# Linear attention and a token/channel mixer in one kernel: the engines' orders and PSUM banks drawn anew for the end of batch 0, batch 1 and the maps of batch 2

## The chip, the core and the metric

The kernel runs on one core of a Trainium2 chip. A core has a matrix engine (TensorE, PE below; its weight loads are listed as PEld), a vector engine (VectorE, DVE), a scalar engine (ScalarE, ACT), a general engine (GpSimd, POOL) and an engine that here only issues transfers (SyncE, SP). Each takes its instructions strictly in the order in which the program gives them; semaphores order them among one another. SBUF is the on-chip memory, PSUM the eight banks of 2 KB in each partition that PE writes its products to. The metric is the device time of one execution in microseconds (us).

## What is computed

Eight batches of 576 rows; q, k and v have 8 heads of 64 columns. Cut to what matters:

```python
def phi(x): return np.where(x > 0, x, np.exp(x) - 1.0) + 1.0
q_p, k_p = phi(q), phi(k)
kv  = einsum('bhsd,bhse->bhde', k_p, v);  z = k_p.sum(axis=2)
x   = (q_p @ kv) / (q_p @ z + 1e-6)            # heads side by side: 576 x 512 a batch
h   = np.maximum(x.T @ w_tok1, 0) @ w_tok2     # mixes rows: 576 -> 256 -> 576
u   = x + h.T
out = u + np.maximum(u @ w_ch1, 0) @ w_ch2     # mixes columns: 512 -> 1536 -> 512
```

Inputs and output are float32; inside, matmuls work on bfloat16.

## The kernel before

One stage follows another for each batch, and the stages of neighbouring batches are interleaved. Every piece of work is a named step; `ORDER` (L64) is the list of all 1085 names, and the loop at the end (L1165) emits them in that order. So it fixes each engine's order: two steps on different engines may stand in either order in the list without a difference, two on the same engine may not. `BANK` (L40) says in which PSUM bank each product lies; two products with one bank can't be in flight together, the second waits until the first has been read.

A name is the batch, the step, and its part. Those that the text uses, n being the batch:

- nLq0, nLk1, nLv0 ...: loads of half of q, k or v, issued by SP (L226, 576 KB each). `GATE` (L32) holds 2Lq0 back until B0 has landed, and 4Lq0 until 2uT1 has.
- nkx0, nqx1: the exponential of phi on ACT (L250); nka0, nqa1: max(x+1, 1) on DVE (L254); nkb0, nqb1: the smaller of both on DVE (L260). There is one buffer for the second (`ybuf`), so nka1 waits for nkb0. nv0, nv1: cast of v (L273), on ACT or, for those in `ON_DVE`, on DVE.
- nK: kv on PE (L300, 72 small matmuls); nKc0, nKc1: its copies on ACT (L306).
- 1Q00 to 1Q11 with 1Qc..: PE transposes of q in batch 1 and their copies (L318, L324); later batches transpose by DMA, nqT0 and nqT1 (L333, SP).
- 1n00 to 1n21 with 1nc..: batch 1's numerator and denominator on PE and the division on DVE (L350, L359 to L362); nn: the same for a later batch in one step of 40 matmuls (L385), divided by nnd, nne, nn0, nn1, nn2, no0, no1 (L398 to L420).
- nf0, nf1 with nfr0, nfr1: first product of the row mixer and its relu on ACT (L446, L450). 1h.. with 1hu.., 1g2 with 1gu2, ng0, ng1 with ngu0, ngu1: its second product and the sum u (L457, L468). 1t0 to 1t3 with 1tc0 to 1tc3: transposes of u by PE; nuT0, nuT1: by DMA (L487).
- 0ma, 0mb, 1ma, 1mb with a number from 0 to 11: the two halves of a map, the first product of the column mixer (L684, two matmuls of 512 columns each). 0r, 1r with the number: its relu on ACT (L693) or DVE (L691). T00 to T02, Tr00 to Tr02: the same for the odd 64 rows of batches 0 and 1.
- 0q0 to 0q11: batch 0's second product of the column mixer (L745, four matmuls of 512 columns). 0z0 to 0z3: sum and output buffer on DVE (L758). 0o0, 0o1: its output transfers, issued by POOL (L762). 0gt, 0gv, 0ut, 0uc: the odd rows.
- From batch 1 (second product) and 2 (first) on, the column mixer is done in seven products of half the size (Winograd's form of Strassen's scheme). np10 to np71: the products (L968), nc, ne, nh: their reading and sums (L1056, L1062, L1069), no: output. nx.., ny..: the maps (L926, L941, L679). nw, ns: sums of the left and right operands on DVE (L834, L883). G01 to G24 (L895) and wt0, wt2 (L822) on DVE, ws00 to ws34 (L814) on POOL: sums of weights, once in the program.
- B0, B1, B2: quarters 1 to 3 of the second weight wc2, loaded and cast by transfers that POOL issues (L1124). B0 waits for the landing of 1Lq0 (L1127). The four quarters of the first weight wc1 are issued at L1119 before the list begins.

The one line of code besides the tables that the change touches is in `load_wc2`.

Of the kernel before, what the change touches and what calls it, by code (L numbers as in the profile page):

```python
# [54 lines left out]

SLOT = {k_: int(v_) for k_, v_ in (e.split(":") for e in """0o0:0 0o1:2 1P:0 V0:4 2P:0 3P:0 V1:4 4P:0 5P:0 6P:0 7P0:4 7t:0 7P1:2""".split())}
# [17 lines left out]
1r0 1ma1 3qa0 1r4 0o0 1ma7 1mb6 wt2 2K 1r6 3qb0 0o1 1mb7 2Kc1 2Kc0 3qa1 1mb1 1r7 2n 1r1 ws24 2nd 3kx0 1ma10
1mb10 2o0 2ne 1ma9 ws34 2n0 1r10 1mb9 3qx1 T00 2o1 2n1 ws30 1r9 1p10 4Lq1 2n2 Tr00 1p11 1w13 1p20 1w10 2f0
3qb1 1w20 3qT1 T01 2fr0 1w23 3ka0 2f1 Tr01 3qT0 3kb0 1c0 1p50 3kx1 G04 G13 1p21 1w40 2fr1 1p51 3v0 G24 2g0
3ka1 1c2 1eZ 1p60 4Lk1 3v1 2gu0 2g1 1hZ 1p61 2gu1 2uT0 1p30 1c1 T02 4qx1 3kb1 2uT1 1w30 1p31 4Lv0 4qa1 3K 1eY
1p71 3Kc0 3Kc1 4qb1 Tr02 1p70 1hY 3n 1eW U00 3ne 1hW 3nd 4Lq0 U01 3n2 4Lv1 4Lk0 U02 3n1 1p41 2s1 3o1 V0 2x01
2x11 2s2 2y01 1p40 3n0 2y11 2x12 4kx1 3o0 1eX 2x16 2x06 2s3 2y16 1o 2x02 2s4 2y06 4qa0 2x21 2x15 2y12 2y21
2x07 4qx0 2y02 2x26 2x05 2y26 2x25 4qb0 2x17 2y25 4ka0 2x27 4qT1 2y05 3f0 2y27 4kx0 2y07 3f1 2y15 4kb0 5Lk0  # L80
3fr0 5Lq0 2x03 2y17 4v0 4qT0 2x13 4ka1 2x23 3fr1 2y03 2x24 5Lk1 2x04 2y13 2y24 2x22 4v1 4kb1 2x14 3gt 2y22
2y04 4K 2y23 2y14 2p10 3gt0 4Kc0 4Kc1 2p11 2w10 5kx0 2w12 3g0 2w20 2c0 2w22 2p20 3gu0 2p21 2p61 3gt1 3uT0 2p60
2w30 3g1 2c1 2eZ 5qx0 2p71 3gu1 2hZ 2p70 4n 3uT1 2eW 2p50 4nd 2w40 3ut 2p51 2p41 4o0 2c2 4n0 5Lv0 2p40 2hW
5Lv1 4n1 2p31 2p30 2eX 3s1 3x01 4o1 3x11 4ne 3y01 3s2 3x02 3y11 2eY 3x21 5kx1 3x06 5ka0 3x16 2hY 4n2 6Lk0 3x12
3y21 3x22 5Lq1 5v0 3y02 3x26 W0 3x05 3s3 3y16 3y12 T12 3y26 5kb0 3y05 2o 3x17 3s4 3y06 3x15 3y22 T11 3y15 5ka1
3x07 3y17 Tr11 6Lk1 3x27 5v1 3y07 3x03 3x25 5kb1 3x13 3y25 3y03 3x14 Tr12 3x04 5qa0 3y14 3x23 3y27 5qx1 6Lq0
4f0 3y23 5qb0 4f1 4fr0 3y13 3x24 5qa1 4fr1 T10 3y24 3y04 3w12 4g0 Tr10 3w10 3p10 5qb1 3p20 3w22 5qT0 4g1 3w20
6kx1 4gu0 3p21 3p50 4uT0 3eZ 3p11 4gu1 3p51 6ka1 U10 4uT1 3c2 3w40 3c0 5K 5qT1 3w30 U11 5Kc0 5Kc1 6kb1 U12
6Lv0 6ka0 7Lk1 3p30 6Lq1 V1 3p31 4s1 3p60 3eY 3p61 4s2 4s3 5n 4s4 3c1 6kx0 5nd 4x11 3hY 3p71 5n0 3p70 7Lk0 3hZ
5o0 5ne 6Lv1 4y11 4x25 3eW 4x21 6qx0 5n2 3hW 3p41 4y21 3p40 5n1 W1 4x01 4y25 5o1 4x26 6kb0 4y01 4x02 4y26 3eX  # L90
4x16 6qx1 4x12 4y02 3o 4x27 6qa1 4x06 4y16 4x15 4y12 4y06 4x17 6qb1 4y15 4x05 6v0 6qa0 4x07 4x23 4y27 5f0 4y05
4y17 4y07 4x03 5fr0 5f1 4y03 7kx1 4y23 4x13 5fr1 6qb0 4x04 4x14 4y13 4y04 6qT1 4x22 4w10 5g1 4y22 6qT0 4x24
4w20 5gu1 4p10 4y24 4p11 4y14 7ka1 6v1 5uT1 5g0 4w12 4p20 4c0 5gu0 7Lq1 5gt 7Lv1 6K 4w22 5uT0 4p50 5gt1 6Kc1
6Kc0 4w30 7kx0 4p21 7Lq0 4p61 7Lv0 5s3 5gt0 4p60 4eZ 5ut 4p51 4c1 4w40 6n 4c2 4hZ 6nd 4p71 6ne 4p70 6o0 6n2
4p30 5s1 4p31 6n0 5x02 4eW 5x01 5x11 4eY 5x12 5y11 6o1 4p41 5s2 5y01 7kb1 5x21 7qx0 5s4 5x06 7ka0 5x16 5y06
4p40 5y12 7F12 5y21 5x07 5y02 5y16 4hY 5x26 4eX 5x15 6n1 5x05 5y15 4hW 5x17 5y26 5x25 5y17 7qx1 5x13 7F13 5x27
5y13 4o 5x14 5y05 7kb0 5x22 5y25 6f0 5y14 5y22 7v0 7qa0 5x03 5y27 5x23 6fr0 6f1 5y07 7v1 7qb0 5x04 6fr1 5y23
5p10 5y03 5x24 7qa1 7K 5y24 5y04 5p11 7qb1 7Kc1 5p20 7Kc0 5w10 7qT1 5c0 5w12 6g0 5w30 7qT0 6g1 5w22 5p21 5w20
6gu0 5p50 5p61 6gu1 6uT0 5p60 5p51 5eZ 5c1 6uT1 5w40 7n 5c2 5p71 5hZ 7nd 5p70 7o0 7n0 5p30 5eW 5p31 7o1 5hW
6x01 7ne 7n1 6x02 6y01 5p40 6s1 5p41 6y02 6s2 6x11 6s3 6x21 6y11 7n2 6x05 6y21 6x06 5eX 6x16 6y06 5eY 6x12  # L100
6y05 6x26 6y12 5hY 6x07 6x22 6x03 6s4 6x15 7F11 6y03 7f0 6y15 7F14 6y07 6y16 7F15 6y22 6x25 6y26 6x13 5o 7fr0
6x17 6y25 6x27 6y17 7f1 7F10 6y13 6y27 6x14 7fr1 6x04 6x23 6y04 6x24 6y14 6w10 6p10 6y24 6y23 7g1 6w12 7g0
7gu1 6p20 6w20 7uT1 6p50 7gu0 6p11 6w22 7gt 7uT0 6c0 6p51 7gt1 6p61 7gt0 6c2 6p60 6w40 7ut 6p21 6c1 7F2 6p31
7s1 7x11 7s2 6p30 6eZ 7x05 6w30 7x21 7x01 6eY 6hZ 6p70 7y01 6p71 6hY 7x02 6eW 7x06 7c4 6hW 7y21 7y11 6p40 7y06
7F3 7x12 7cr4 6p41 7y12 7x26 7s3 7x15 6eX 7y26 7c1 7y02 7y15 6o 7y05 7s4 7x16 7F4 7c2 7y16 7cr1 7x07 7cr2 7x17
7y07 7x13 7y17 7x22 7x25 7y22 7x14 7y25 7y13 7x27 7y14 7x04 7y27 7x03 7y04 7w12 7x23 7y03 7c3 7w22 7y23 7c5
7w10 7w42 7x24 7cr5 7w20 7c0 7cr3 7w40 7w32 7y24 7p11 7cr0 7w14 7p20 7w34 7w24 7p10 7R11 7p51 7R10 7p61 7R51
7w44 7p50 7R61 7ts1 7p21 7R50 7R20 7p60 7w30 7ta2 7R21 7ts2 7p31 7D210 7p71 7R31 7t5 7D311 7ts3 7R71 7ta1
# [5 lines left out]
def kernel(  # L114
# [44 lines left out]
    def bank(name):  # L159
        return psum[:, BANK[name]]  # L160

    def banks(name, m=2):
        return psum[:, BANK[name]:BANK[name] + m]

# [50 lines left out]
    def after(ins, other):  # L215
        if other is not None:
            tc.add_manual_dep(ins.ins, other.ins.name, sync_dep, reason="order of transfers")
        return ins
# [17 lines left out]
    def put(name, fn, *a):  # L236
        assert name not in tok, name
        tok[name] = lambda: fn(*a)

    live = {}  # L240
# [35 lines left out]
    for n in range(1, B):  # L276
        for c in range(2):
            put(f"{n}v{c}", vcast, n, c, dve if f"{n}v{c}" in ON_DVE else act)

# [110 lines left out]
    def nd_tile(n, m):  # L390
        return banks(f"{n}n{m}")[:, :, 0:D1 * 7].rearrange("p i (k e) -> p i k e", k=7)

    def nd_den(n):
        at = BANK[f"{n}n0"]
        assert BANK[f"{n}n1"] == at + 2
        nd_tile(n, 0), nd_tile(n, 1)
        both = psum[:, at:at + 4, 0:D1 * 7].rearrange("p b (k e) -> p b k e", k=7)
        nc.vector.tensor_scalar(out=dens.rearrange("p m i k -> p (m i) k"), in0=both[:, :, :, D],  # L398
                                scalar1=EPS, scalar2=None, op0=ALU.add)
        nc.vector.reciprocal(out=dens, in_=dens)  # L400
# [287 lines left out]
    def mm3_read(n, mc):  # L688
        o, ps = cr[n % 2][:, mc, :], bank(f"{n}m{mc}")
        if f"{n}r{mc}" in ON_DVE:  # L690
            nc.vector.tensor_scalar(out=o, in0=ps, scalar1=0.0, scalar2=None, op0=ALU.max)  # L691
# [504 lines left out]
```

## Time and profile before

| what | us |
|---|---|
| three runs | 249.63, 249.79, 248.96; median 249.63 |
| the profiled execution | 249.09 |
| its span, first to last instruction | 247.3 |
| PE busy in 22 to 35, 35 to 40, 40 to 62 us | 13.00, 3.62, 22.00 |
| PE busy in 62 to 68, 68 to 104 us | 5.21, 35.30 |
| DVE busy in the same five stretches | 8.54, 4.45, 20.45, 5.86, 35.16 |

A matmul's record holds its whole passage through the array and the records overlap, so busy time says that PE was never empty, and the distance from one start to the next says how fast it went. The steps that the change moves run from about 20 us (the loads of batch 1) to about 89 us (the maps of batch 2, step 2x12 on PE). The landings of single loads in the text are the trace's semaphore events, step names are put to the trace's rows engine by engine in the order of the program.

### The profile page before, as it was taken

What the parts mean: (1) busy time and instruction counts of PE and PEld (TensorE: products, weight loads), DVE (VectorE), ACT (ScalarE), POOL (GpSimd) and SP (SyncE); (2) the same over time, 40 slices, a digit from 0 to 9 for tenths busy, and PEclk for the clock granted to TensorE, in tenths of its full rate; (3) what the DMA queues carried; (4) which work ended last, traced back from release to release, by engine and by line L of the source; (5) the groups of instructions that cost most, each with busy time, mean ns of one, the idle gap of its engine ahead of it and who ended that gap; (6) DMA issues with size and microseconds to landing.
All of it is one profiled execution on the core that took longest, in us unless ns stands there. A gap on an engine that the chain in (4) does not pass through costs nothing.

```text
span 247.3 us, 6399 instructions
## 1 busy us (share of the span) xinstructions
PE 235.2 (95%) x2616; PEld 174.3 (70%) x2616; DVE 214.4 (87%) x387; ACT 136.2 (55%) x224; POOL 81.2 (33%) x88
## 2 busy tenths in 40 slices
PE   7899998999899999899999999999999999999992
PEld 3585444464577686789866786778778877888881
DVE  5956698899999999989999899989999869869862
ACT  4771891487947289537962496717832462274100
POOL 9870043373902420036100460024305430630360
PEclk9999999999999999999999999999999999999998
DMA  6999949999958999967967986892654075125035
GB/s 243 271 203 248 366 165 205 405 353 243 376 154 160 219 297 172 289 139 237 362 211 150 312 265 160 197 279 84 132 129 94 0 154 105 21 52 121 3 79 176
DMA packets 49805, 48.42 MB, mean 196 GB/s; under 512 B 30064, under 2 KB 35568, under 8 KB 49776
## 3 DMA queue, kind: packets, MB, share of 16 engines
q1 hardware_dynamic: 41664, 35.00, 49.9%
q0 software_dynamic: 7472, 12.22, 24.0%
q10 hardware_dynamic: 640, 0.79, 1.2%
q8 instruction: 20, 0.33, 0.6%
q14 instruction: 9, 0.07, 0.1%
HBM read 35.85 MB, written 9.44 MB: 183 GB/s over the span
## 4 chain that ended last, share of the span: by engine, by line
PE 60%; DVE 6%; DMA 5%; issue 2%; ACT 0%; SPq 0%; DVEq 0%
PE ps L926 21%; PE ps L968 21%; PE ps L446 5%; PE ps L457 3%; DMA uT<-u 3%; PE ps L731 2%; DMA qT<-qp 2%; DVE u L468 2%; PE ps L1022 2%; PE ps L709 2%; PE ps L385 1%; PE ps L745 1%; PE ps L300 1%; DVE y L254 1%; DVE x L411 1%
## 5 line engine op out<-in xcount | busy, mean ns | idle before, releaser
L968 PE MATMUL ps<-k_raw,v_raw 128*128 128x256 bf16 x252 | 31.5, 273 | 0.8 <-DVE ut L481 0.8
L941 ACT COPY v_raw<-ps 128x512 f32<-128x512 f32 x30 | 17.0, 592 | 26.0 <-PE ps L926 22.2
L1069 POOL TENSOR_TENSOR obuf<-obuf,q_raw 128x512 f32<-128x512 f32 x6 | 9.4, 1563 | 62.2 <-DVE obuf L1062 47.6
L968 PEld LDWEIGHTS <-cr 128*128 128x128 bf16 x252 | 24.5, 98 | 5.4 <-issue 0.9
L968 PEld LDWEIGHTS <-v_raw 128*128 128x128 bf16 x252 | 24.2, 98 | 5.2 <-issue 1.4
L926 PEld LDWEIGHTS <-swc 128*128 128x128 bf16 x240 | 23.4, 98 | 3.8
L926 PEld LDWEIGHTS <-wc 128*128 128x128 bf16 x216 | 21.0, 98 | 4.2 <-DMA uT<-u 0.5
L679 DVE CUSTOM_DVE_ANT_0 cr<-ps,v_raw 128x512 bf16<-128x512 f32 x30 | 20.2, 685 | 4.0 <-PE ps L926 3.9
L250 ACT ACTIVATE e<-q_raw 128x1152 bf16<-128x1152 f32 x16 | 18.7, 1167 | 8.0 <-DMA q_raw<-in_q_dram 7.9
L926 PE MATMUL ps<-crt,swc 128*128 128x256 bf16 x180 | 22.7, 273 | 0.0
L684 PE MATMUL ps<-uT,wc 128*128 128x512 bf16 x96 | 22.2, 379 | 0.0
L968 PE MATMUL ps<-wc,cr 128*128 128x256 bf16 x168 | 21.5, 273 | 0.8 <-DVE x L411 0.8
L250 ACT ACTIVATE e<-k_raw 128x1152 bf16<-128x1152 f32 x16 | 18.7, 1167 | 4.2 <-DMA k_raw<-in_k_dram 4.1
L926 PE MATMUL ps<-uT,wc 128*128 128x256 bf16 x144 | 19.8, 273 | 0.5 <-DVE x L411 0.3
L1069 POOL TENSOR_TENSOR obuf<-obuf,w 128x512 f32<-128x512 f32 x6 | 8.4, 1405 | 30.5 <-ACT w L1056 20.7
L1062 DVE TENSOR_TENSOR obuf<-ps,u 128x512 f32<-128x512 f32 x24 | 16.3, 684 | 1.7 <-PE ps L968 1.4
L411 DVE TENSOR_TENSOR x<-ps,dens 128x768 bf16<-128x768 f32 x18 | 16.6, 940 | 0.0
L834 DVE TENSOR_TENSOR v_raw<-cr 128x512 bf16<-128x512 bf16 (+3 forms) x24 | 14.9, 640 | 2.0 <-ACT cr L939 1.8
L684 PEld LDWEIGHTS <-wc 128*128 128x128 bf16 x96 | 9.0, 98 | 10.3 <-issue 1.0
L468 DVE TENSOR_TENSOR u<-ps,x 128x1024 bf16<-128x1024 f32 x12 | 14.5, 1219 | 0.7 <-PE ps L457 0.7
L446 PE MATMUL ps<-x,w 128*128 128x512 bf16 x56 | 14.4, 379 | 0.0
L260 DVE TENSOR_TENSOR qp<-e,y 128x1152 bf16<-128x1152 bf16 x16 | 13.0, 814 | 1.5 <-ACT e L250 1.2
(168 smaller groups left out, 511.8 us busy)
## 6 DMA issues: line engine op xcount, KB each, us to landing
k_raw<-in_k_dram SPq DMA_DIRECT2D x16, 576.0 KB, 5.9
q_raw<-in_q_dram SPq DMA_DIRECT2D x16, 576.0 KB, 6.1
v_raw<-in_v_dram SPq DMA_DIRECT2D x14, 576.0 KB, 6.9
out_dram<-obuf POOLq DMA_DIRECT2D x12, 512.0 KB, 6.5
wc<-in_moe_w_ch_dram POOLq DMA_DIRECT2D x8, 384.0 KB, 10.2
out_dram<-obuf POOLq DMA_DIRECT2D x4, 256.0 KB, 6.3
cr<-in_v_dram POOLq DMA_DIRECT2D x2, 288.0 KB, 7.0
out_dram<-obuf POOLq DMA_DIRECT2D x4, 128.0 KB, 5.2
```

Source lines behind the costliest of these rows:

```text
L250: nc.scalar.activation(out=ebuf[EBUF[f"{n}{nm}{c}"]], in_=f, func=AF.Exp)
L411: nc.vector.tensor_tensor(out=xv[:, :, rc0:rc0 + 3], in0=nd_tile(n, m)[:, :, k0:k0 + 6, 0:D].rearrange("p i (q a) d -> p i q a d", a=2), i ...
L446: nc.tensor.matmul(out=banks(f"{n}f")[:, mt], lhsT=w1t[:, b, ms] if r == R else w1[:, r, ms], rhs=x[b][:, r, :], start=(r == 0), stop=(r = ...
L468: nc.vector.tensor_tensor(out=u[b][:, rs], in0=banks(f"{n}g{i}"), in1=x[b][:, rs], op=ALU.add)
L679: nc.vector._custom_dve(TENSOR_ADD_SAT, out=o, in0=ps, in1=c, s0=3.4028234663852886e38, s1=0.0)
L684: nc.tensor.matmul(out=bank(f"{n}m{mc}"), lhsT=wc1[:, kj, 128 * mc:128 * mc + 128], rhs=uTj[b][:, kj] if n < 2 - U1 else uT[b][:, :, kj], ...
L834: return engine.tensor_tensor(out=s_[which - 1][:, ks], in0=x_, in1=y_, op=op)
L926: nc.tensor.matmul(out=ps[:, j], lhsT=lhs[:, k_, 128 * j:128 * (j + 1)], rhs=rhs[:, :, k_], start=(first and j == 0 and k_ == 0), stop=(k_ ...
L941: nc.scalar.copy(out={1: c1, 6: c6, 5: c5}[i], in_=ps)
L968: nc.tensor.matmul(out=ps, lhsT=lhs[:, k_], rhs=rhs[:, k_], start=(first and not skip and k_ == 0), stop=(k_ == KH - 1), skip_group_check= ...
L1062: nc.vector.tensor_tensor(out=slots(f"{n}P", 4)[:, d::2, HC[c]], in0=pair_tile(n, "X" if z == "W" else z), in1=u[n % 2][:, d::2, HC[c]], o ...
L1069: nc.gpsimd.tensor_tensor(out=o, in0=o, in1=part[i], op=ALU.add)
```

## The change

The tables are redrawn and one condition is taken from a table. `ORDER` has the same 1085 names. On PE the order changes from 0ma7 to 1p40, on DVE from G01 to 1eX, on ACT from 0r1 to 2y01, on SP from 1Lv0 to 4Lk0, on POOL from ws12 to 1hW. Behind these each engine has its old order. 51 entries of `BANK` get another bank, all of batches 0 and 1, of batch 2's projection, row mixer and first maps, and 3K.

`WGATE` holds the condition that L1127 held, and its one entry is the same landing, 1Lq0's.

```diff
+WGATE = {1: ('in', 'q', 1, 0)}
...
-BANK: 2K:1 2n0:1 2n1:3 2n2:5 2f:6 2g0:2 2g1:6 3K:6 1h00:4 1h01:7 1h10:0 1t0:4 1t1:3 1t2:7 1t3:6 1Q0:4 1Q1:6 1K:5 1n10:4
+BANK: 2K:3 2n0:0 2n1:2 2n2:4 2f:4 2g0:5 2g1:3 3K:5 1h00:3 1h01:5 1h10:4 1t0:5 1t1:1 1t2:1 1t3:7 1Q0:6 1Q1:6 1K:4 1n10:6
...
-            live["in", "q", 1, 0] if i == 1 else None)
+            live[WGATE[i]] if i in WGATE else None)
```

(`BANK` is cut to the entries that the text comes back to.) The order of each engine, before and after, from the first difference on; a plain word stands for a step, `..` for a run of steps as before:

```
PE before  0ma7 0ma4 0ma3 0mb3 0ma5 0ma8 0mb1 0mb5 0mb0 0mb4 0mb8 0ma2 0ma6 0mb6 0ma9 0mb7 0mb2 0ma11 0ma10 0mb10
           0mb11 0gt 0mb9 0q1 1K 0q0 1Q00 1Q01 0q2 1n10 1Q10 1Q11 0q3 1n00 0q4 1n20 0q5 0q6 1n01 0q7 1n11 0q8 1n21 0q9
           1f0 0q10 1f1 0q11 1h00 1h01 1h11 1h10 1t0 1t1 1g2 1t2 1t3 1ma2 1ma8 1ma0 0ut 1mb8 1ma4 1ma11 1ma3 1mb11 1mb3
           1ma5 1mb5 1mb0 1mb2 1ma6 1mb4 1ma1 1ma7 1mb6 2K 1mb7 1mb1 2n 1ma10 1mb10 1ma9 1mb9 T00 1p10 1p11 1p20 2f0 T01
           2f1 1p50 1p21 1p51 2g0 1p60 2g1 1p61 1p30 T02 1p31 3K 1p71 1p70 3n U00 U01 U02 1p41 2x01 2x11 1p40 2x12
PE after   0ma5 0ma4 0mb0 0ma3 0mb3 0mb5 0mb4 0ma9 0mb1 0mb9 0ma11 0ma2 0mb2 0ma7 0mb7 0mb11 0gt 0ma8 0mb8 0ma6 0ma10
           0mb10 0q0 0q1 1Q00 1Q01 0mb6 0q2 1Q10 1Q11 1K 0q3 1n00 1n20 0q4 0q5 1n10 0q6 1n01 0q7 1n11 0q8 1n21 0q9 0q10
           1f0 1f1 0q11 1h01 1h00 1h10 1h11 1t1 1t0 1g2 1t3 1t2 1ma3 1ma9 1ma2 0ut 1ma10 1mb3 1ma7 1ma1 1mb1 1mb9 1mb7
           1mb10 1ma8 1ma4 1mb4 1mb2 1mb8 2K T00 1ma11 1mb11 2n 1ma5 1ma6 1mb6 1mb5 1ma0 1p20 1mb0 T02 2f0 1p10 2f1 1p11
           1p50 1p51 2g1 1p21 2g0 1p60 1p61 1p31 1p30 T01 3K 1p71 1p70 3n U00 1p41 U01 U02 2x11 2x01 1p40 2x12
DVE before 0r3 G01 1ka0 G21 0r6 1kb0 1ka1 1v0 1kb1 0gv 0r9 G22 1qa0 1qb0 G11 1qa1 G12 1qb1 G03 1nc10 1Qc10 1Qc11 1nc00
           1nc20 G23 wt0 1nc01 1nc11 1nc21 2qa0 2qb0 2qa1 2qb1 0z0 0z2 1hu01 1hu11 1tc0 0z1 1gu2 1tc2 0z3 2ka0 G14 G02
           2kb0 2ka1 2v1 2kb1 1r5 1r8 3qa0 wt2 3qb0 3qa1 2nd 2o0 2ne 2n0 2o1 2n1 2n2 1w13 1w10 3qb1 ..
DVE after  0r3 G11 G21 G23 G01 G22 1ka0 1kb0 0r9 G12 0gv 1ka1 1kb1 1qa0 1qb0 1qa1 1v0 1qb1 0r6 1Qc10 1Qc11 1nc20 1nc00
           1nc10 1nc01 1nc11 2qa0 1nc21 2qb0 G03 2qa1 2qb1 0z0 0z3 0z2 1hu01 1hu11 1tc0 0z1 1gu2 1tc2 2ka0 2kb0 2ka1 wt2
           2v1 2kb1 3qa0 1r8 wt0 3qb0 3qa1 2nd 2o1 2n1 2ne 2n0 2n2 2o0 1r5 1w10 1w30 1w13 1w20 3qb1 3ka0 1w23 G13 3kb0
           G02 1w40 3ka1 2gu1 G04 2gu0 3kb1 1eY G24 4qa1 1eZ 4qb1 1eW 3nd 3ne 3n0 3n2 3n1 2s1 3o1 2s2 V0 G14 3o0 1eX
ACT before 0r1 0r0 1kx0 0r8 0r5 0r4 0r7 0r2 1kx1 0r10 0r11 1v1 1qx0 1Kc0 1Kc1 1qx1 1Qc00 1Qc01 2qx0 1fr0 2qx1 1fr1 2kx0 ..
ACT after  0r0 0r4 0r5 1kx0 0r1 0r2 0r7 1kx1 1qx0 0r10 0r11 0r8 1qx1 1Qc01 1Qc00 1v1 1Kc1 1Kc0 2qx0 2qx1 2v0 1fr0 1fr1 2kx0 ..
SP before  1Lk0 1Lk1 1Lv0 1Lv1 1Lq0 1Lq1 2Lq0 2Lq1 2Lk0 2Lk1 2Lv1 3Lq0 2Lv0 3Lq1 2qT0 2qT1 3Lk0 3Lk1 3Lv1 3Lv0 4Lq1 3qT1
           3qT0 4Lk1 2uT0 2uT1 4Lv0 4Lq0 4Lv1 4Lk0 4qT1 5Lk0
SP after   1Lk0 1Lk1 1Lq0 1Lq1 1Lv0 1Lv1 2Lq0 2Lq1 2Lv0 2Lk0 3Lq0 2Lk1 3Lq1 2Lv1 2qT1 2qT0 3Lk0 3Lv0 3Lk1 3Lv1 4Lq1 3qT0
           3qT1 2uT1 2uT0 4Lk0 4Lk1 4Lq0 4Lv1 4Lv0 4qT1 5Lk0
POOL before B0 B1 B2 ws02 ws04 ws12 ws22 ws00 ws32 ws14 ws10 ws20 0o0 0o1 ws24 ws34 ws30 1hZ 1hY 1hW 1o
POOL after  B0 B1 B2 ws02 ws04 ws14 ws12 ws00 ws22 ws10 ws24 ws20 0o0 0o1 ws34 ws30 ws32 1hZ 1hW 1hY 1o
```

## The prediction

> **What bounds the kernel now.** I read the page first, then who TensorE (PE) waits for between 22 and 104 us, then its timeline at the waits, then the chain of waits, then the timelines of VectorE (DVE) and GpSimd (POOL).
>
> ```profile
> span 247.3 us, 6399 instructions
> PE 235.2 (95%) x2616; PEld 174.3 (70%) x2616; DVE 214.4 (87%) x387; ACT 136.2 (55%) x224; POOL 81.2 (33%) x88
> ```
>
> PE is busy for 95%, at a granted clock of 1.00 in every window up to 200 us. A redrawn order over the same instructions can win only where PE stands still in the part that is redrawn. Its timeline, 34 to 40 us:
>
> ```profile
> 34.21 1.04 PE L745 MATMUL ps<-wc,cr 128*128 128x512 bf16 x4
> 35.57 0.68 PE L318 MATMUL ps<-identity,qp 128*128 128x128 bf16 x9 [0.32 <-DVE qp L260]
> 36.08 1.03 PE L745 MATMUL ps<-wc,cr 128*128 128x512 bf16 x4
> 37.82 0.41 PE L350 MATMUL ps<-kvbd,qT 128*128 128x130 bf16 x4 [0.71 <-ACT qT L324]
> 38.06 0.67 PE L318 MATMUL ps<-identity,qp 128*128 128x128 bf16 x9
> 39.08 1.02 PE L745 MATMUL ps<-wc,cr 128*128 128x512 bf16 x4 [0.35 <-DMA wc<-in_moe_w_ch_dram]
> ```
>
> The columns are start, length, and in brackets idle time and releaser. Matmuls overlap, so I count from start to start: in an unbroken run, 512 columns take 0.216 us (five in 1.08 in the chain below), 128 columns 0.054. Four that start at 34.21 are through at 35.07, the next starts at 35.57: 0.50 lost. In the same way 0.88 before 37.82 and 0.53 before 39.08. The three waits are 1Q00 for 1qb0 on DVE, 1n10 for 1Qc01 on ScalarE (ACT), and 0q3 for the landing of B0. The fourth wait is in the chain:
>
> ```profile
> 62.40 1.73 DVE qp L260
> ...
> 64.18 1.49 issue
> ...
> 66.87 0.82 DVE x L411
> ...
> 67.73 2.13 PE ps L968 x18
> ...
> 71.83 1.08 PE ps L446 x5
> ```
>
> 1p10 waits for 2n0. T00 (16 x 0.054 from 65.89) is through at 66.77, 1p10 starts at 67.73: 0.96 lost. Its cause stands four instructions earlier on DVE:
>
> ```profile
> 62.40 1.71 DVE L260 TENSOR_TENSOR qp<-e,y 128x1152 bf16<-128x1152 bf16 x1
> 64.15 1.60 DVE L254 TENSOR_SCALAR y<-q_raw 128x1152 bf16<-128x1152 f32 x1
> ```
>
> These are 3qb0 and 3qa1; their like take 0.75 and 0.76, so 0.96 and 0.84 too long. POOL at that time:
>
> ```profile
> 59.83 1.16 POOL L814 TENSOR_TENSOR q_raw<-wc,q_raw 128x512 f32<-128x512 bf16 x1 [5.44 <-DVE kp L260]
> 60.94 2.60 POOL L762 DMA_DIRECT2D out_dram<-obuf  x4
> 63.55 4.34 POOL L814 TENSOR_TENSOR q_raw<-wc,q_raw 128x512 f32<-128x512 bf16 x3
> ```
>
> The first and second of the last three took 1.58 and 1.57 instead of 1.16: DVE's work from SBUF and POOL's exclude one another. Of 19 DVE operations from SBUF beside POOL's DMA issues, 3qb0 alone is long. Two short waits (for 1gu2 and 0z3 near 54 us) cost 0.21. From 68 to 103 us PE loses nothing; DVE is busy 35.2 of 36 us there.
>
> **The change, part by part.** No instruction is added or removed, and from 2x12 PE's order is the old one. I add the rows' own durations along each engine's new order: map pair halves 0.43, 0q 0.86, phi_add and phi_end 0.75, phi_exp 1.17, L691 0.69, map reads on ACT 0.60, group sums 0.42, casts 0.77 on DVE and 1.17 on ACT; a reader starts about 0.59 after the start of a 0.43 pair. An operation behind an independent one on DVE or ACT overlaps it by 0.08 to 0.11.
>
> *Loads.* 1Lq0, 1Lq1 go ahead of 1Lv0, 1Lv1. By position 1Lq0 lands at 30.5 (1Lv0 did) instead of 33.5; it gates B0, which POOL issued 0.5 after it, so B0 to B2 move up by 3 us, and behind B0 all of SP's 2L loads. B0 then meets 1Lv0 and 1Lv1 still in flight. Bounds for 1Lv1: 34.9 as the last load had, if B0 waits; 37.1 if they share as loads and weights did between 22 and 30 us (about 200 and 90 KB per us by their packets, against 410 and 200 alone: of the loads 2.2 us at 410 are left when B0's packets begin at 32.7, 2.2 after its gate as before; at 200 that is 4.4 us). 1v1 on ACT is due at 36.69; from 37.15 it ends at 38.32, 0.46 later, and 1K's second half waits for it. Price 0 or 0.46. Sharing is the nearer row: I take 0.46. B0 itself, due at 38.4, lands between 37.1 and 38.3: no wait.
>
> *Maps of batch 0.* 0ma9 and G11 now come first of those that need the last quarter of wc1, landed 25.98. PE reaches 0ma9 at 22.23 + 7 x 0.432 = 25.25 and waits 0.79 with the release. G11 starts at 26.02, and from there DVE has no gap above 0.5: four more group sums and 1ka0 to 28.46, 1kb0 29.24, 0r9 29.83, G12 30.17, 0gv 31.36 (0gt starts at 30.02), 1ka1, 1kb1 32.82, 1qa0, 1qb0 34.39. Meanwhile PE does 22 more halves, 0gt, 0q0 and 0q1 and stands at 1Q00 at 34.44. ACT, in order, ends 0r10 33.53, 0r11, 0r8 34.52: 1Q00 starts 34.57, 0.13 lost. Then 1Q01, 0mb6, 0q2 to 36.38. 1Q10 now shares banks with 1Q00, so it waits for 1qx1 (35.59), 1Qc01 and 1Qc00 (36.79) on ACT as well as 1qb1 (36.53): 0.46 lost. 1K starts 37.35; its second half waits 0.1 for 1v1. Together 1.48 lost against 1.91: with 1n00 and the hand-offs, 1h01 starts at 49.53 where 1h00 did at 49.94, **0.41 gained**. Between them the six rounds 1n and 1nc hang behind 0q blocks that cover them by 0.4 or more; 2v0 stands before 1fr0 and 1fr1 on ACT and costs nothing while 2Lv0 lands before 47.1 (estimate 46.1 to 47.2; each us later costs one).
>
> *Maps of batch 1.* 0z3 precedes 0z2, so neither 1gu2 (53.97) nor 0z3 is waited for: **0.21 gained**. POOL's ws00 to ws24 lie at 49.1 to 53.7, beside DVE work from PSUM, which it doesn't slow in any row.
>
> *Batch 2's projection.* 2n starts at 62.81 (before 63.41 with 0.03 more work done). DVE before it: 2kb1 ends 58.90, 3qa0 59.69, then 0.66 idle until 1mb8 releases 1r8 at 60.35; wt0 61.9, 3qb0 62.58, 3qa1 63.37. 2nd can start at 63.46: DVE is just in time, with no cover. 2n1 now leads: 0.17+0.04+0.33+0.03+0.29-0.08+0.95 puts its end at 65.19, and PE, with 1ma5, 1ma6, 1mb6, 1mb5 kept back as filler, needs it for 1ma0 at 65.28. 2n2 and 2o0 are done at 67.44, 2f0 comes at 67.7. The 0.96 is gone: **0.96 gained** if 3qb0 and 3qa1 take 0.75. If they don't, the loss passes one to one. Bounds 0 and 1.80 (0.96+0.84, as before); most rows beside POOL's issues show 0, and ws20 is over at 60.8, wt0 begins at 60.95: I take 0.
>
> [...]
>
> *Down to 2x12.* DVE gets 1r5, G02 and G14 here, 0.69+0.34+0.34 less a pipelined overlap, 1.29 in all. From 2nd at 63.46 its sum reaches 1eZ at 80.67 (3n due 80.6), 3n2 84.5 (2x11 due 84.75), 3o1 85.9 (86.3), 3o0 87.4 (87.6), 1eX 88.0 (88.45). No wait over 0.1, but cover is only 0.2 to 0.5. 2gu1 goes before 2gu0, so 2uT1 and with it 4Lq0 leave some 2.6 us earlier; 4Lk0 and 4Lk1, now ahead of 4Lq0, cost under 3 us by their 1.4 us each. At 103 us 2p61 waits 0.94 for 2c0, behind 5kx0, behind the landing of 5Lk0: all of that is released from work that moves up, so the wait stays and the gain passes.
>
> **The sum.** 0.41 + 0.21 + 0.96 - 0.46 = 1.12 us. The span of 247.3 becomes 246.2; the profiled run took 249.09, 1.8 around its span, and becomes 248.0. The median, 249.63, lies 0.54 above the profiled run; against it I forecast **248.5**.
>
> **Rivals.** (1) 3qb0 is held 0.96 again: 1.12 - 0.96 = 0.16, 249.5. For: same neighbours, POOL's four issues at 60.8 to 63.4 over wt0 and 3qb0. Against: 18 other rows. [...] (3) The gain is lost at 103 us because 5Lk0 lands when it did (102.16): 249.6. Against: its issue waits for 4ka0, 4kx0 and 4qT1, which all move.
>
> **How the numbers follow.** Forecast 0.52, (1) 0.12, (2) 0.28, (3) 0.08; (2) takes in other waits that use up the thin covers. What tells no change from a change is 0.3%, 0.75 us: the forecast is faster, (1) and (3) the same, (2) slower. Alone the forecast spans 248.0 (no sharing of B0's transfer, 1.58) to 248.9. The range: below, 1.58 and half of the wait at 103 us, 249.63 - 2.05 = 247.6; above, rival (2), 250.8.
>
> **What would show it.** 0ma9 waits 0.7 to 0.8 for wc1; no wait at 1n10 or 0q3; 1Q10 waits for ACT's 1Qc00; 1Lv1 lands at 37 and 1v1 holds 1K's second half; 3qb0 and 3qa1 at 0.75; 1ma0 without a wait; about 0.9 at 2p61. It would be wrong if 3qb0 is long again, if wc1's last quarter lands well after 26 us (every us there costs one), if 2Lv0 lands after 47, or if PE waits for DVE between 68 and 90 us.

## The result and the profile after

Twelve runs of each kernel: the changed kernel has a median of 250.50 us (249.73 to 252.17), the one before 249.50 (248.29 to 250.01). The ratio is 1.0053, with a 95% interval from 1.0031 to 1.0076: the change made the kernel slower by 1.3 us on the mean (1.0 between the medians), where 1.1 us of gain had been forecast. The profiled run of after took 250.83 us around a span of 249.1.

The first lines of the page. 20 of PE's 2616 matmul records are missing here, so PE's busy share is not to be compared with before; the starts of the records that are there can be.

```profile
span 249.1 us, 6380 instructions
PE 233.2 (94%) x2596; PEld 174.0 (70%) x2616; DVE 216.0 (87%) x387; ACT 136.4 (55%) x224; POOL 80.8 (32%) x88
```

PE's timeline, the places that were shown of before, and the new ones (start, length, idle time and releaser in brackets):

```profile
22.06 3.19 PE L686 MATMUL ps<-uT,wc 128*128 128x512 bf16 x14
26.54 1.69 PE L686 MATMUL ps<-uT,wc 128*128 128x512 bf16 x7 [1.29 <-DMA wc<-in_moe_w_ch_dram]
...
35.18 0.68 PE L320 MATMUL ps<-identity,qp 128*128 128x128 bf16 x9
...
37.31 0.68 PE L320 MATMUL ps<-identity,qp 128*128 128x128 bf16 x9 [0.16 <-DVE qp L262]
...
63.93 1.68 PE L686 MATMUL ps<-uT,wc 128*128 128x512 bf16 x7
68.51 0.59 PE L686 MATMUL ps<-uT,wc 128*128 128x512 bf16 x2 [2.89 <-DVE x L413]
```

Counted from start to start, as in the prediction: 0ma9 waits 1.46 for the last quarter of wc1, 1Q00 0.21, 1Q10 0.33 (for 1qb1 on DVE). The waits for 1Qc01 and for B0 of before are gone. Taken together this is a small gain: 1h01 starts at 49.83, where 1h00 started at 49.94 before. Then comes the largest wait of the execution: the four halves from 1ma5 to 1mb5 are eight matmuls, start at 63.93 and are through at 65.66, and 1ma0 starts at 68.51. **2.85 us are lost** where 0.96 was lost before, and 0 was forecast. The row above has only seven of the eight: one record is missing, and the weight load that follows each matmul's start stands at 65.45 for it too. A second execution of the same kernel (after_again, below) has all eight, and loses the same 2.85 from 65.11 on:

```profile
63.38 1.90 PE L686 MATMUL ps<-uT,wc 128*128 128x512 bf16 x8
67.96 1.01 PE L686 MATMUL ps<-uT,wc 128*128 128x512 bf16 x2 [2.68 <-DVE x L413]
```

Where the expectations below have 3.06 or 3.1 for this wait, seven matmuls were counted. 2x12, from which PE's order is the old one, starts at 89.46 (87.83 before); 3gt at 100.01 (98.38): the shift of 1.63 made here goes through to the end, where the span is 1.8 longer.

The cause stands on DVE, in the same two operations as before. DVE's timeline, then POOL's:

```profile
59.70 0.76 DVE L256 TENSOR_SCALAR y<-q_raw 128x1152 bf16<-128x1152 f32 x1
...
61.35 0.96 DVE L824 TENSOR_TENSOR k_raw<-wc 128x1536 bf16<-128x1536 bf16 x1
62.23 1.72 DVE L262 TENSOR_TENSOR qp<-e,y 128x1152 bf16<-128x1152 bf16 x1
63.98 2.83 DVE L256 TENSOR_SCALAR y<-q_raw 128x1152 bf16<-128x1152 f32 x1
66.73 0.17 DVE L400 TENSOR_SCALAR dens<-ps 128x28 f32<-128x28 f32 x1
```

```profile
59.81 1.67 POOL L816 TENSOR_TENSOR q_raw<-wc,q_raw 128x512 f32<-128x512 bf16 x1 [5.83 <-DVE kp L262]
61.44 2.44 POOL L764 DMA_DIRECT2D out_dram<-obuf  x4
63.90 3.93 POOL L816 TENSOR_TENSOR q_raw<-wc,q_raw 128x512 bf16<-128x512 bf16 x3
```

3qb0 takes 1.72 and 3qa1 2.83, where their like take 0.75 and 0.76: 0.97 and 2.07 too long. 2n is through at 63.9, but 2nd, which reads it, starts only at 66.73, behind 3qa1. Beside 3qb0 POOL issues the four stores of 0o0 and 0o1; beside 3qa1 it computes ws34 (63.90 to 65.07 in the trace) and ws30 (65.02 to 66.18), with no gap between them.

### The profile page after: what moved, and what is told of

Same layout as the page of the kernel before. It is cut to its first block, busy times and chain, and to the rows that moved or that the text cites. A ratio compares the mean times of both kernels' runs of the same rounds, so it can differ in the third digit from the quotient of the medians.

```text
span 249.1 us, 6380 instructions
## 1 busy us (share of the span) xinstructions
PE 233.2 (94%) x2596; PEld 174.0 (70%) x2616; DVE 216.0 (87%) x387; ACT 136.4 (55%) x224; POOL 80.8 (32%) x88
## 4 chain that ended last, share of the span: by engine, by line
PE 71%; DMA 14%; DVE 8%; issue 3%; POOL 2%; ACT 0%; SPq 0%; DVEq 0%; POOLq 0%
PE ps L928 21%; PE ps L970 21%; PE ps L448 6%; DMA wc<-in_moe_w_ch_dram 6%; PE ps L686 5%; PE ps L747 4%; PE ps L459 3%; DMA cr<-in_v_dram 3%; DMA uT<-u 3%; PE ps L733 2%; DMA qT<-qp 2%; DVE u L470 2%; PE ps L1024 2%; PE ps L711 2%; DVE y L256 1%
## 5 line engine op out<-in xcount | busy, mean ns | idle before, releaser
L695 ACT ACTIVATE cr<-ps 128x512 bf16<-128x512 f32 x19 | 10.5, 602 | 10.8 <-PE ps L686 10.8
L256 DVE TENSOR_SCALAR y<-q_raw 128x1152 bf16<-128x1152 f32 x16 | 14.2, 888 | 0.2
```

The costliest lines, as they stand in the source:

```text
L256: nc.vector.tensor_scalar(out=ybuf[YBUF[f"{n}{nm}{c}"]], in0=f, scalar1=1.0, scalar2=1.0, op0=ALU.add, op1=ALU.max)
```

## The experiments

Theory A: the 3 us belong to POOL's sums ws34 and ws30, which 3qb0 and 3qa1 have to wait for. Theory B: the two operations are long for another reason (chance, their place, the DMA issues). Theory C: the stall is covered, or what is won there is lost behind it. All runs below are of the changed kernel with one edit, unless said otherwise; the ratios are to the kernel before, with 95% intervals.

**The same kernel again.**

> The changed kernel once more, unedited, to see what of its profile repeats. Theory A (the DVE stall at batch 2's projection is in the order itself): 3qb0 takes about 1.7 us and 3qa1 about 2.8 us again, PE stands about 3.1 us before 1ma0, ratio to the kernel before 1.005. Theory B (a chance of one execution): one of the two is near 0.76 us and the wait before 1ma0 is under 1.5 us. The landing of wc1's last quarter (25.98 us in the profile of before, 26.49 in that of after) tells at the same time whether the wait of 0ma9 is a matter of the execution or of the order: it should lie between 25.5 and 26.7 us.

Ratio 1.0072 (1.0044 to 1.0100). 3qb0 takes 1.72, 3qa1 2.82, PE waits 2.85 before 1ma0, as in after: the stall is in the order. wc1's last quarter landed at 25.94, and 0ma9 waited 0.78; over all thirteen profiles of this study it landed between 25.47 and 27.42. That part is a matter of the execution.

**POOL's sums held back.**

```diff
-        first = {(0, 0): ("phi", "q", 2, 1), (2, 0): ("phi", "k", 2, 1)}.get((i, k0))
+        first = {(0, 0): ("phi", "q", 2, 1), (2, 0): ("phi", "k", 2, 1), (3, 4): ("add", "q", 3, 1)}.get((i, k0))
```

phi_add notes its instruction under ("add", nm, n, c), and ws34 waits for that of 3qa1. The runs below that change this line note the instruction waited for in the same way.

> The changed kernel, with POOL's ws34 held back until 3qa1 is done, so that no POOL arithmetic runs beside 3qa1. Theory A (ws34 and ws30, back to back, hold 3qa1): 3qa1 falls from 2.83 to 0.76 us, 2nd starts 2.07 us earlier, PE's wait before 1ma0 falls from 3.06 to about 1.0 us, 3qb0 stays at 1.72; the time falls by 2.07 us against the changed kernel, to a ratio of 0.997 to the kernel before. Theory B (3qa1 is long for a reason of its own): 3qa1 stays near 2.8 us, ratio 1.005. Theory C (the stall has cover elsewhere): 3qa1 is short, but PE waits somewhere behind, and the ratio stays above 1.002.

Ratio 0.9937 (0.9914 to 0.9961): better than forecast, since 3qb0 is short too. DVE and POOL in this run:

```profile
61.23 0.74 DVE L262 TENSOR_TENSOR qp<-e,y 128x1152 bf16<-128x1152 bf16 x1
62.01 0.85 DVE L256 TENSOR_SCALAR y<-q_raw 128x1152 bf16<-128x1152 f32 x1
62.92 0.19 DVE L400 TENSOR_SCALAR dens<-ps 128x28 f32<-128x28 f32 x1
```

```profile
60.43 2.54 POOL L764 DMA_DIRECT2D out_dram<-obuf  x4
63.01 3.40 POOL L816 TENSOR_TENSOR q_raw<-wc,q_raw 128x512 bf16<-128x512 bf16 x3
```

The four DMA issues lie beside 3qb0 exactly as in after (they begin 0.80 before it, 0.79 there), and it takes 0.74. So the issues alone do not hold it; 3qa1, beside the last of them, is 0.09 longer than its like. 2nd starts with 2n's end, and 1ma0 has no wait. Theories B and C fall.

**The issues moved away as well** (`0o0 0o1` behind `ws32` in ORDER, on top of sums_wait).

> As sums_wait, and the four issues of the stores 0o0 and 0o1 stand behind ws32 on POOL instead of beside 3qb0, so that POOL does nothing from the end of ws20 (61.5 us) until 3qa1 is done. Theory A (the DMA issues hold 3qb0): 3qb0 falls from 1.72 to 0.76 us, PE's wait before 1ma0 is under 0.2 us, the time is 0.97 us below sums_wait and 3.0 below the changed kernel: a ratio of 0.993 to the kernel before. Theory B (3qb0 is long in this place whatever POOL does): 3qb0 stays at 1.7 us and the time is that of sums_wait, 0.997.

Ratio 0.9963 (0.9934 to 0.9992). 3qb0 takes 0.74 and 3qa1 0.76 (0.85 in sums_wait): there is next to nothing left to win. The 0.97 that was expected from this step had already come with the sums.

**A control: a wait that is over early** (ws34 waits for 1r8).

```diff
-        first = {(0, 0): ("phi", "q", 2, 1), (2, 0): ("phi", "k", 2, 1)}.get((i, k0))
+        first = {(0, 0): ("phi", "q", 2, 1), (2, 0): ("phi", "k", 2, 1), (3, 4): ("r", 1, 8)}.get((i, k0))
```

> A control of sums_wait: the changed kernel with the same kind of wait before ws34, but for DVE's 1r8, which is done (61.4 us) before 3qb0 starts. Theory A (it is the sum standing ready behind the DMA issues that holds 3qb0 and then 3qa1): nothing changes against the changed kernel, 3qb0 1.7 us, 3qa1 2.8 us, ratio 1.005 to 1.007. Rival (any wait at this place breaks POOL's run of instructions and lets DVE in): 3qb0 and 3qa1 are short or halved, and the ratio is near sums_wait's 0.994.

Ratio 1.0088 (1.0057 to 1.0119), 3qb0 1.71, 3qa1 2.84, a wait of 2.85 before 1ma0. It is not the wait instruction that helps, but that no sum stands ready.

**The same edit in the old order** (ws24 waits for 3qa1, in the kernel before).

```diff
-        first = {(0, 0): ("phi", "q", 2, 1), (2, 0): ("phi", "k", 2, 1)}.get((i, k0))
+        first = {(0, 0): ("phi", "q", 2, 1), (2, 0): ("phi", "k", 2, 1), (2, 4): ("add", "q", 3, 1)}.get((i, k0))
```

> The kernel before, with POOL's ws24 held back until 3qa1 is done: the one edit of sums_wait, in the old order. Theory A (POOL's sums hold 3qb0 and 3qa1 in both orders): both fall to 0.76 us, PE's wait of 0.96 us before 1p10 goes, the time falls by 0.96 us, a ratio of 0.996. What then remains between this and sums_wait is what the redrawing is worth without the stall: 0.6 us by the prediction's other terms (0.41 + 0.21), so sums_wait should be 0.2 to 0.3% below this. Rival (the old order did not suffer from the sums, the wait before 1p10 has another cause): ratio 1.000.

Ratio 0.9959 (0.9942 to 0.9975), 1.0 us. 3qb0 takes 0.75 and 3qa1 0.94, and 1p10 follows T00 without a wait (66.89, 0.89 after T00's start). So the old order lost its 0.96 to the same sums. Without the stall the redrawn order stands at 0.9937 (0.9963 with the issues moved as well) against 0.9959. The intervals overlap, so whether the redrawing is worth anything apart from this place is not shown.

**The sums set apart by a semaphore** (ws30 waits for ws34, ws32 for ws30).

```diff
-        first = {(0, 0): ("phi", "q", 2, 1), (2, 0): ("phi", "k", 2, 1)}.get((i, k0))
+        first = {(0, 0): ("phi", "q", 2, 1), (2, 0): ("phi", "k", 2, 1), (3, 0): ("ws", 3, 4), (3, 2): ("ws", 3, 0)}.get((i, k0))
```

> The changed kernel with ws30 waiting for ws34 and ws32 for ws30 by semaphore, so that POOL's three sums no longer overlap by 0.05 us but stand some 0.1 us apart, as ws24 and ws34 did in the kernel before. Theory A1 (sums that run into each other never give DVE a gap; with a gap DVE gets in after one): 3qa1 falls from 2.83 to about 1.65 us, 3qb0 stays at 1.72, PE's wait before 1ma0 falls from 3.06 to about 1.9 us, the time falls by 1.2 us, a ratio of 1.000 to 1.002. Rival A2 (DVE waits for two sums because two were queued): 3qa1 stays at 2.8 us or is longer, ratio 1.005 to 1.007.

Ratio 1.0003 (0.9983 to 1.0024), as expected: 3qa1 1.72, PE's wait 1.74.

```profile
61.26 1.72 DVE L262 TENSOR_TENSOR qp<-e,y 128x1152 bf16<-128x1152 bf16 x1
63.01 1.72 DVE L256 TENSOR_SCALAR y<-q_raw 128x1152 bf16<-128x1152 f32 x1
```

With a gap of 0.07 between the sums (64.11 to 64.18 in the trace) 3qa1 is held by one of them instead of two, and 1.1 us of the wait are gone. In the changed kernel ws34 is followed by ws30, which does not depend on it, without a gap; before, ws24 was followed by ws34, which does, with a gap of 0.08.

**DVE's side instead** (`3qb0 3qa1` behind `1r5`, with 3kx1 and 4Lq1 moved likewise).

```diff
-3qx1 2K 1r8 0o0 1r2 T00 wt0 2Kc0 2Kc1 1ma11 3qb0 Tr00 0o1 1mb11 1r4 3qa1 2n 1r11 4Lq1 2nd 1ma5 ws34 1ma6 2o1
-2n1 1mb6 1mb5 ws30 1r6 2ne 1ma0 2n0 3kx1 1p20 ws32 2n2 1mb0 T02 1r0 2o0 1r5 3kx0 2f0 1w10 1w30 3v0 1p10 1w13
-2f1 Tr02 1w20 3qb1 1p11 2fr1 3ka0 3qT0 1p50 2fr0 1w23 1c0 1p51 G13 3v1 3qT1 3kb0 2g1 G02 1c2 1p21 1w40 2g0
+3qx1 2K 1r8 0o0 1r2 T00 wt0 2Kc0 2Kc1 1ma11 Tr00 0o1 1mb11 1r4 2n 1r11 2nd 1ma5 ws34 1ma6 2o1
+2n1 1mb6 1mb5 ws30 1r6 2ne 1ma0 2n0 1p20 ws32 2n2 1mb0 T02 1r0 2o0 1r5 3qb0 3qa1 4Lq1 3kx0 2f0 1w10 1w30 3v0 1p10 1w13
+2f1 Tr02 1w20 3qb1 1p11 2fr1 3ka0 3qT0 1p50 2fr0 1w23 1c0 1p51 G13 3v1 3qT1 3kb0 2g1 G02 1c2 3kx1 1p21 1w40 2g0
```

> The changed kernel with DVE's 3qb0 and 3qa1 moved behind 2n's readers (2nd to 1r5), and ACT's 3kx1 and SP's 4Lq1, which wait for them, moved likewise; POOL's order is untouched. Nothing between 2n and 1ma0 then reads SBUF on DVE but the short reciprocals. Theory A: 2nd starts within 0.2 us of 2n's end, 2n1 ends near 65.3 us, PE's wait before 1ma0 is under 0.3 us, and the time is 2.8 to 3.1 us below the changed kernel, a ratio of 0.993 to 0.994 to the kernel before. Theory C (what DVE does not do here it does later, and PE waits for 1w10 to 1w23 or for ws32 instead): less than 1.5 us come back, ratio above 0.999.

A miss: ratio 1.0009 (0.9981 to 1.0037). The wait before 1ma0 is gone as expected (1ma0 at 65.15), but PE stands again from 77 us on:

```profile
77.63 1.05 PE L711 MATMUL ps<-uTt,wc 128*128 128x128 bf16 x16
79.10 0.48 PE L302 MATMUL ps<-vs,kp 64*64 64x65 bf16 x36 [0.41 <-DVE u L470]
79.77 0.48 PE L302 MATMUL ps<-vs,kp 64*64 64x65 bf16 x36 [0.18 <-DVE kp L262]
82.06 0.79 PE L387 MATMUL ps<-kvbd,qT 64*128 64x65 bf16 x40 [0.40 <-DVE obuf L1064]
```

DVE now sits idle for 1.61 ahead of 2nd and has 1.5 us more to do behind it, in a stretch where it has no cover: PE waits 0.31 for 2gu1 ahead of T01, and 0.41, 0.18 and 0.40 for 2gu0, 3kb1 and 1eZ. Theory C holds for this way of mending it, though PE waits at other steps than it named; it does not hold for the other way.

**Why 3qb0?** In after the trace shows no sum beside 3qb0; ws34's span begins behind the four issues. Either the span is late, and ws34 is at work long before it begins (theory S), or the span is right, and a sum that only stands ready is enough (theory R).

```diff
-        first = {(0, 0): ("phi", "q", 2, 1), (2, 0): ("phi", "k", 2, 1)}.get((i, k0))
+        first = {(0, 0): ("phi", "q", 2, 1), (2, 0): ("phi", "k", 2, 1), (3, 4): "wt0"}.get((i, k0))
```

> The changed kernel with ws34 waiting for DVE's wt0, which ends (62.30 us) after 3qb0 has started (62.23) and well before the profile shows ws34 (63.90, behind the four DMA issues). It asks why 3qb0 is held although the profile shows no sum beside it. [...] Theory R (the span is right, ws34 starts behind the issues, and what holds 3qb0 is that ws34 stands ready when 3qb0 comes): 3qb0 takes 0.76 us and 3qa1, done at 63.8, meets no sum; no wait before 1ma0, ratio 0.994.

Ratio 0.9981 (0.9958 to 1.0003). 3qb0 goes free, and 3qa1 is held by 0.85, from 62.77 on, though ws34's span begins only at 63.65:

```profile
61.99 0.75 DVE L262 TENSOR_TENSOR qp<-e,y 128x1152 bf16<-128x1152 bf16 x1
62.77 1.61 DVE L256 TENSOR_SCALAR y<-q_raw 128x1152 bf16<-128x1152 f32 x1
```

```profile
61.20 2.44 POOL L764 DMA_DIRECT2D out_dram<-obuf  x4
63.65 3.97 POOL L816 TENSOR_TENSOR q_raw<-wc,q_raw 128x512 bf16<-128x512 bf16 x3
```

PE waits 0.66 before 1ma0. Theory R had no hold on 3qa1 and no wait here, so this looked like theory S. The next run asked the sum itself when it was over; by S that is before 3qa1 is:

```diff
-GATE = {'1k0': ('wc1', 0), '2q0': ('wc2', 1), '4q0': ('u', 2, 1), '7q0': ('u', 5, 1)}
+GATE = {'1k0': ('wc1', 0), '2q0': ('wc2', 1), '4q0': ('u', 2, 1), '7q0': ('u', 5, 1), '4q1': ('ws', 3, 4)}
```

> A look at when ws34 is really over: sums_wait_wt0, with SP's load 4Lq1, which already waits for 3qa1, made to wait for ws34 as well. In the profile of sums_wait_wt0 3qa1 ends at 64.38, 4Lq1 follows it by 0.06 to 0.1, and ws34's span ends at 65.39. [...] Theory R (the span is right): 4Lq1 is issued about 1.0 us after 3qa1's end, 0.06 to 0.1 after the end of ws34's span. 3qa1 takes 1.6 us in both; the time is that of sums_wait_wt0, 247.5 to 250.

SP's load, then DVE's 3qa1 and POOL's ws34 to ws32 in that run:

```profile
65.53 0.37 SPq L228 DMA_DIRECT2D q_raw<-in_q_dram  x1
```

```profile
62.89 1.60 DVE L256 TENSOR_SCALAR y<-q_raw 128x1152 bf16<-128x1152 f32 x1
```

```profile
63.77 3.99 POOL L816 TENSOR_TENSOR q_raw<-wc,q_raw 128x512 bf16<-128x512 bf16 x3
```

In this one run (248.51 us) 3qa1 is over at 64.50, and the load goes out at 65.53, 1.03 later and 0.02 after ws34's span ends (65.51 in the trace). The span is right as to its end, and ws34 was not over before 3qa1: S falls. R had expected, in the run before, that 3qa1 would not be held at all, and falls too. What stays is that 3qa1 was held for 0.84 while POOL's last issues went out and ws34 stood ready behind them; whether ws34 had begun by then, the end of its span does not tell.

**The sums in a row, with no issues before them** (`0o0 0o1` behind `ws32`, no wait added).

```diff
-3qx1 2K 1r8 0o0 1r2 T00 wt0 2Kc0 2Kc1 1ma11 3qb0 Tr00 0o1 1mb11 1r4 3qa1 2n 1r11 4Lq1 2nd 1ma5 ws34 1ma6 2o1
-2n1 1mb6 1mb5 ws30 1r6 2ne 1ma0 2n0 3kx1 1p20 ws32 2n2 1mb0 T02 1r0 2o0 1r5 3kx0 2f0 1w10 1w30 3v0 1p10 1w13
+3qx1 2K 1r8 1r2 T00 wt0 2Kc0 2Kc1 1ma11 3qb0 Tr00 1mb11 1r4 3qa1 2n 1r11 4Lq1 2nd 1ma5 ws34 1ma6 2o1
+2n1 1mb6 1mb5 ws30 1r6 2ne 1ma0 2n0 3kx1 1p20 ws32 0o0 0o1 2n2 1mb0 T02 1r0 2o0 1r5 3kx0 2f0 1w10 1w30 3v0 1p10 1w13
```

> The changed kernel with the four issues of 0o0 and 0o1 behind ws32 and no wait added: ws20, ws34, ws30 and ws32 stand in a row on POOL from 59.8 us. If each sum that runs into the next keeps DVE out for its length (0.97 to 1.11 us of 1.16), the three that follow ws20 hold DVE's work from SBUF by 3.0 to 3.3 us in all, wherever they fall (on wt0 or 3qb0 instead of on 3qb0 and 3qa1): PE's wait before 1ma0 is 2.9 to 3.4 us and the ratio 1.005 to 1.008, as in the changed kernel. If the DMA issues are a part of the stall (rival), 0.9 us of it go with them: ratio 1.001 to 1.003.

Ratio 0.9999 (0.9977 to 1.0020), PE's wait 1.62. Here neither expectation held:

```profile
60.66 0.97 DVE L824 TENSOR_TENSOR k_raw<-wc 128x1536 bf16<-128x1536 bf16 x1
61.55 1.71 DVE L262 TENSOR_TENSOR qp<-e,y 128x1152 bf16<-128x1152 bf16 x1
63.30 1.60 DVE L256 TENSOR_SCALAR y<-q_raw 128x1152 bf16<-128x1152 f32 x1
```

wt0 comes first and is free, 3qb0 is held by 0.97 and 3qa1 by 0.84: in this run the two engines take turns, one sum, one operation of DVE, and in the trace each sum that meets one takes 1.67 to 1.87 instead of 1.16. The row of sums did not hold DVE for its whole length. Of the 3.04 that 3qb0 and 3qa1 lose in after, taking the issues out from in front of the sums gave 1.24 back; taking the sums away, in sums_wait, gave 2.96.

**A version better than both.** sums_wait, and two more edits for waits that the profiles show:

```diff
-0ma4 0mb0 0ma3 0r0 0mb3 0mb5 0r3 0mb4 G11 0ma9 0r4 G21 0mb1 G23 0r5 0mb9 G01 G22 0ma11 1kx0 1ka0 0ma2 0mb2 0r1
-0ma7 1kb0 0mb7 0r2 0r9 0mb11 0r7 G12 0gt 1kx1 0ma8 0gv 0mb8 1ka1 0ma6 1qx0 B0 0ma10 1kb1 0mb10 B1 0q0 1qa0
+0ma4 0mb0 0ma3 0r0 0mb3 0mb5 0r3 0mb4 1ka0 G01 G11 0r4 G21 0mb1 0ma2 0mb2 0ma7 0mb7 G23 0r5 0ma9 0mb9 G22 0ma11 1kx0 0r1
+1kb0 0r2 0r9 0mb11 0r7 G12 0gt 1kx1 0ma8 0gv 0mb8 1ka1 0ma6 1qx0 B0 0ma10 1kb1 0mb10 B1 0q0 1qa0
-2y23 2y14 2p10 4Kc0 3gt0 4Kc1 2p11 2w10 2w12 5kx0 3g0 2w20 2w22 2p20 2c0 3gu0 2p21 2p61 3gt1 3uT0 2p60 2w30
+2y23 2y14 2p10 4Kc0 3gt0 4Kc1 2p11 2w10 2w12 3g0 2w20 2w22 2p20 2c0 5kx0 3gu0 2p21 2p61 3gt1 3uT0 2p60 2w30
```

> sums_wait with two more edits, each for a wait that its profile and that of after show: on PE 0ma2, 0mb2, 0ma7 and 0mb7 (which need earlier quarters of wc1) stand before 0ma9, with 1ka0 and G01 before G11 on DVE, so that neither engine waits for wc1's last quarter (0.34 to 1.46 us in five profiles); and on ACT 5kx0 stands behind 2c0, so that 2p61 does not wait for the landing of 5Lk0 (1.03 us in sums_wait). If both waits end there: 0.3 to 0.5 and 1.0 us less than sums_wait, a ratio of 0.987 to 0.989 to the kernel before. Rivals: 1Q00 and 1Q10 wait for ACT and DVE by as much longer as 0ma9 waits less, since the quarter's readers are late anyway (then 0.990); or 4n waits for 2c1's followers and the 1.0 us stays (0.992 to 0.994).

Ratio 0.9861 (0.9835 to 0.9887), 245.83 us in four runs: 3.5 us below the kernel before, 1.9 below sums_wait, more than the two edits were priced at. Both waits are gone:

```profile
22.09 6.21 PE L686 MATMUL ps<-uT,wc 128*128 128x512 bf16 x28
...
99.27 1.47 PE L970 MATMUL ps<-wc,cr 128*128 128x256 bf16 x12
100.58 1.47 PE L970 MATMUL ps<-k_raw,v_raw 128*128 128x256 bf16 x12
```

28 matmuls of the maps run through without a wait for wc1, and 2p61 (100.58) follows 2p21 at once, where PE lost 1.03 in sums_wait.

## Why the prediction was wrong

- **The step that failed** is the term for batch 2's projection: "0.96 gained if 3qb0 and 3qa1 take 0.75 [...] most rows beside POOL's issues show 0 [...] I take 0." That 3qa1 and POOL's sums lengthen one another, as the prediction read from their rows, is shown: 3qa1 takes 2.83 in after, 0.85 with the sums held back (sums_wait), 2.84 in its control (sums_wait_early); in the old order it falls from 1.60 to 0.94 (before_sums_wait). It does not hold for every DVE instruction on SBUF: the reciprocal of 2nd's result, at 65.88 beside ws34 in before, kept its 0.33. But 3qb0's 0.96 in the old profile was read as an effect of the issues beside it, and since 18 of 19 operations beside issues were not long, it was taken for an exception. What the runs show to matter is what stood behind the issues: with a sum ready there 3qb0 takes 1.72 (after), with none 0.74 (sums_wait). And 3qa1 was not put on the clock against POOL's list: ws20 was not over at 60.8 but, held by 3qa0, at 61.48; the issues ran to 63.88 and ws34 and ws30 to 66.18, all over 3qa1. The prediction had DVE just in time here "with no cover", and so it was: of the 3.04 us that the two operations lost, well over its bound of 1.80, 2.85 passed on to PE. The term was -1.89 (0.96 less 2.85) instead of +0.96.
- **Rival (2)**, slower at 250.8, is what happened, with a price too small. The 2.30 us of waiting in its figure are 0.50 on 3qa0, 0.96 on 3qb0 and 0.84 on 3qa1; measured were 0.97 on 3qb0 and 2.07 on 3qa1. The 0.50 no run shows: in after 3qa0 takes 0.76, and ws20 beside it 1.67 instead of 1.16. The total, 1.18 us slower, comes near the measured 1.3, but partly by chance: the wait was 0.55 longer than its 2.30, and the 0.46 for B0's transfer was not paid. That two sums could pass a waiting operation was in no row of before. Which of the two engines waits was not the same each time: ws20, which came 0.11 after 3qa0, took the wait itself; 3qa1, which had started at 63.98, was passed by ws30 at 65.02; and 3qb0 was held while the trace shows no sum.
- **Maps of batch 0**: right in kind, a size off. 0ma9 waits for the last quarter, 0.79 forecast, 1.46 in after because the quarter landed at 26.49, 0.78 in after_again with a landing like that of before. 1Q00 0.21 (0.13 forecast), 1Q10 0.33 (0.46), released by 1qb1 on DVE and not, as forecast, by 1Qc00 on ACT. No wait at 1n10 or 0q3, as forecast. 0.11 gained in after, 0.65 in after_again, 0.41 forecast.
- **Sharing of B0's transfer, 0.46**: not paid. 1Lv1 landed at 35.06, at the bound that had been set aside (34.9); B0 took the delay, 6.0 us from issue to landing (31.03 to 37.04) against 5.0 before (34.01 to 39.03), and was not waited for.
- **Maps of batch 1, 0.21**: gained; 1gu2 and 0z3 are not waited for.
- **Down to 2x12**: "no wait over 0.1, but cover is only 0.2 to 0.5" was nearly right: 0.15 at 3n for 1eZ. dve_2n_first shows how little cover there was.
- **The wait at 103 us** passes through as forecast: 1.14 in after, 0.59 to 1.21 in the other runs that keep ACT's order there. In best, with 5kx0 behind 2c0, it is gone.

Without the stall the sum is about right: sums_wait is 1.6 us (1.0 to 2.1) below the kernel before; the forecast was 1.12, or 1.58 without the 0.46 that was not paid. That is for the sum as a whole: most of it is the 0.96, and the smaller terms are not shown one by one.

## What to carry to other kernels

An operation that is long once among many of its kind has something that the others lack: look at what is queued on the neighbour's list, not only at what runs beside it. Where a vector operation from SBUF stands on the critical path, lay GpSimd's list on the clock over it, with each of its instructions as long as it takes when held (here up to 1.87 for a sum of 1.16), and give GpSimd's work a wait that ends after the operation; that costs nothing if its results are needed later. Here holding the sums back was worth more (0.9937) than moving the vector work behind it (1.0009), as the vector engine had no cover there.

## What the runs showed of the hardware that was not expected

**A hold with no sum in the trace.** With a sum ready behind POOL's DMA issues, DVE's next operation from SBUF (3qb0 in after, after_again, before, sums_apart and sums_wait_early, 3qa1 in sums_wait_wt0 and sum_end) is held by 0.84 to 0.97, about as long as by a real sum, although the sum's span lies behind the issues (a semaphore confirms its end to 0.02). wt0 or wt2, which lies beside the first two issues, is free each time (0.95 to 0.97). With the same issues and no sum ready 3qb0 is free as well (0.74 in sums_wait and best, 0.75 in before_sums_wait). What holds DVE there stays open, and so does why ws30 passed the waiting 3qa1 in after, when in sums_in_a_row DVE got its turn after every sum.

**A lower clock after a long wait.** Three profiles have the wait of 2.85 us before 1ma0, and in two of them, after_again and sums_wait_early, PE's granted clock was lower behind it; in after it was not. The stretches of after_again, of sums_wait_early, then those of after (from and to, length, PE busy and matmuls, granted clock, DMA share, GB/s):

```profile
62.00:68.00 6.00, 3.32 (x53) 0.99 0.83 297
68.00:72.00 4.00, 4.00 (x27) 0.59 0.35 126
72.00:80.00 8.00, 8.00 (x59) 1.00 0.31 76
```

```profile
62.00:68.00 6.00, 4.56 (x118) 1.00 1.04 405
68.00:72.00 4.00, 2.49 (x13) 0.79 0.51 166
72.00:80.00 8.00, 7.95 (x60) 0.89 0.29 70
```

```profile
62.00:68.00 6.00, 3.56 (x58) 1.00 0.89 330
68.00:72.00 4.00, 3.49 (x32) 1.00 0.39 145
72.00:80.00 8.00, 7.95 (x61) 1.00 0.31 76
```

By these means the lower clock took 1.70 us of full clock in after_again (6 x 0.01 + 4 x 0.41) and 1.72 in sums_wait_early (4 x 0.21 + 8 x 0.11). In after_again 1ma0's two matmuls take 0.81 from start to start instead of 0.43 in after, and 2f0 comes 4.03 after 1ma0 instead of 2.40: the wait cost 1.63 more. Why the clock stayed at 1.00 in after, behind a wait of the same length, is not shown. Over all timed runs, 14 of the 32 of the three kernels with this wait (after, after_again, sums_wait_early) had a mean granted clock of 0.993 or less, and none of the 60 of sums_wait, sums_wait_puts_late, sums_wait_wt0, sums_apart and sums_in_a_row (dve_2n_first, without the wait as well, has 2 of 12), so a part of the change's loss is likely the clock's.
